# Banks for the first q and u, and the order of work at the change of row blocks, in a fused GELU feed-forward forward and backward kernel

## The chip, the cores and the metric

The kernel runs on one core of one Trainium2 chip, as a single launch. Its time is device microseconds (us) of that core; the number compared is the median of repeated runs. Beside the times there is one profiled execution, from which all durations of single instructions come.

## The reference

One feed-forward layer with an approximate (tanh) GELU, and its gradients, in bf16:

```python
h   = x @ w1 + b1            # x [2048, 448], w1 [448, 1792]
out = gelu(h) @ w2 + b2      # w2 [1792, 448]
# vjp with grad_out [2048, 448]:
gh  = (grad_out @ w2.T) * gelu'(h)
gx  = gh @ w1.T;  gw1 = x.T @ gh;  gb1 = sum(gh)
gw2 = gelu(h).T @ grad_out;        gb2 = sum(grad_out)
```

The outputs are out, gx, gw1, gb1, gw2 and gb2.

## The kernel before

The 2048 rows are four blocks of 512 (`NB`), the 1792 hidden columns seven pairs of 128-wide tiles (`NPAIR`). One **step** g is one pair of hidden tiles in one row block, so there are 28 steps and seven steps to a block; step 7 is the first of block 1. All is transposed: hidden columns lie on the partitions, rows along the free dimension. The order of instructions on each engine is the order in which the Python code issues them (a manual schedule); the engines meet only through semaphores, which the tile framework puts in where a tile is written after a read or read after a write.

In a step g the engines do this, by the names that the profile's lines use:

- TensorE makes `u` = w1.T x for step g+2 (`M1`, L239, six matmuls, and L249 in `rest`, one 64-row matmul for each half), `q` = w2 grad_out.T for step g (L252 in `rest`, then `M4`, L258, six matmuls), and between them **pieces** (L406): single matmuls of the out and gx products, each for one `Unit`, which is 128 rows of out ("o") or gx ("g") and accumulates over 14 pieces.
- ScalarE (`act_first`, `act_second`) copies u with its bias into `V` (L285, two instructions, which free u), squares it into `A` (L286), writes gelu into `hT` (L287), and takes tanh of `Bt` (L357). It also evicts some units (L420).
- VectorE (`dve_first`, `dve_second`, `dve_gate`) makes `Bt` from A and V (L354), p from A and hT (L361), adds constants to t and p (L362, L363), multiplies them (L364), and the **gate** multiplies by q into `ghT` (L375), which frees q. It also evicts the other units of out, adding b2 (L422).
- GpSimd issues the stores of finished units (L426) and of hT to a DRAM scratch (L379), and makes a few copies (L163). SyncE issues the loads and the transposes of ghT.

PSUM has eight banks of 128 x 512 float32: `psum_u` holds one tile `u` of two banks, `psum_g` one tile `q` of two banks, `psum_a` four tiles `acc` of one bank. The pools have one, one and four buffers, so that the next u waits until ScalarE has copied the last one, the next q until the gate has read the last one, and a new accumulator until one of four is evicted or read. V, A and Bt exist once. V may be written again when Bt has been made.

Step 0 is cut into two halves of 256 rows, so that it can begin when half of x has landed. `first_products` makes its u: the first half in two acc tiles, the second half in one q tile (`ub`, two banks). `first_chain` runs ScalarE (L311 copy, L316, L320, L323) and VectorE (L312 copy, L326, L330, L332, L335, L336) over the halves. Then TensorE issues M1 and rest of step 1, three matmuls that keep it busy (L279), and `first_q` (L271): one q tile whose two banks hold the two row halves, with one more such matmul between them. The gate of step 0 (L371) is two instructions, one for each half, on that one tile.

Block 0 has four out units under way (`grow[0]`), whose accumulators are finished at step 6, the last of block 0. Units 0 and 1 are evicted by ScalarE at step 6, after the pieces; units 2 and 3 by VectorE at step 7, ahead of the gate. At step 7 the kernel runs four pieces of two new out units (`grown`), then M1 of step 9, then eight pieces of gx (`own`):

```python
        flush(False); dve_gate(g); act_first(nxt); flush(True); dve_first(nxt)
        act_second(nxt); dve_second(nxt)
        if g == NPAIR:
            run_pieces(grown); M1(g + 2); run_pieces(own)
```

From step 6 on, each step ends with up to two stores of hT. After the 28 steps the last block's units are finished, and the weight gradients follow (L569, L577, L588), with the sums for gb1 and gb2 on VectorE and GpSimd.

Of the kernel before, what the change touches and what calls it, by code (L numbers as in the profile page):

```python
# [11 lines left out]
F32 = mybir.dt.float32  # L12
# [6 lines left out]
def kernel(  # L19
# [15 lines left out]
    nc = tc.nc  # L35
    P = 128
# [10 lines left out]
    SB = 512  # L47
    NB = S // SB
    SPB = SB // P
    NPAIR = NF // 2  # L50
    assert DL == 64 and F % 256 == 0 and S % SB == 0 and NPAIR == 7 and NB == 4
    NSTEP = NB * NPAIR
# [11 lines left out]
    psum_u = ctx.enter_context(tc.tile_pool(name="psum_u", bufs=1, space=bass.MemoryType.PSUM))  # L64
    psum_g = ctx.enter_context(tc.tile_pool(name="psum_g", bufs=1, space=bass.MemoryType.PSUM))
    psum_a = ctx.enter_context(tc.tile_pool(name="psum_a", bufs=4, space=bass.MemoryType.PSUM))
# [23 lines left out]
    w2T_sb = w2T_flat.rearrange("p (k f) -> p k f", k=KD)  # L90
# [12 lines left out]
    def gq(b):  # L103
        o = ((b % 2) * 2 + 1) * KD * SB
        return xg_flat[:, o:o + KD * SB].rearrange("p (k s) -> p k s", k=KD)
# [5 lines left out]
    def hT(g):  # L111
        return ring(hT_flat, HR, g)
# [4 lines left out]
    def V_of(g):  # L117
        return VA_flat[:, 0:2 * SB].rearrange("p (h s) -> p h s", h=2)

    def A_of(g):  # L120
        return VA_flat[:, 2 * SB:4 * SB].rearrange("p (h s) -> p h s", h=2)
# [4 lines left out]
    def t_of(g):  # L126
        return ring(T_flat, 4, 2 * (g % 2))

    def p_of(g):
        return ring(T_flat, 4, 2 * (g % 2) + 1)  # L130
# [8 lines left out]
    HB = SB // 2  # L139
# [84 lines left out]
    def cols(g, h):  # L224
        c = g % NPAIR
        return slice((2 * c + h) * P, (2 * c + h + 1) * P)

    u_of = {}
    g_of = {}

    def M1(g):
        if g == 0:
            u_of[g] = [psum_a.tile([P, SB], F32, name="acc")[:] for h in range(2)]
        else:
            u = psum_u.tile([P, 2, SB], F32, name="u")
            u_of[g] = [u[:, h, :] for h in range(2)]
        for h in range(2):
            for kt in range(KF):
                nc.tensor.matmul(u_of[g][h], lhsT=w1_sb[:, 1 + kt, cols(g, h)], rhs=xq(g // NPAIR)[:, 1 + kt, :],  # L239
                                 start=(kt == 0), stop=False, skip_group_check=True)  # L240
# [20 lines left out]
    def first_q():  # L261


        q = psum_g.tile([P, 2, SB], F32, name="q")
        g_of[0] = q
        for r in range(2):
            rs = slice(r * HB, (r + 1) * HB)
            for kt in (KF, *range(KF)):
                ps = slice(0, DL if kt == KF else P)
                for h in range(2):  # L270
                    nc.tensor.matmul(q[:, r, h * HB:(h + 1) * HB], lhsT=w2T_sb[ps, kt, cols(0, h)], rhs=gq(0)[ps, kt, rs],  # L271
                                     start=(kt == KF and h == 0), stop=(kt == KF - 1),
                                     tile_position=(0, 0) if kt == KF else None, skip_group_check=True)
            if r == 0:
                keep_warm(1, w1_sb[:, 1, 0:P], xq(0)[:, 1, :])
# [2 lines left out]
        for i in range(n):  # L278
            nc.tensor.matmul(pw[:], lhsT=weights, rhs=moving, start=True, stop=True)  # L279

    def act_first(g):
        u = u_of.pop(g)
        for h in range(2):
            ft = 2 * (g % NPAIR) + h
            nc.scalar.activation(out=V_of(g)[:, h, :], in_=u[h], func=ACT.Identity, bias=b1_col[:, ft:ft + 1])  # L285
        nc.scalar.activation(out=A_of(g), in_=V_of(g), func=ACT.Square, scale=math.sqrt(3.0 * GELU_C * GELU_A))  # L286
        nc.scalar.activation(out=hT(g), in_=V_of(g), func=ACT.Gelu_apprx_tanh)  # L287

    def first_products():

        ub = psum_g.tile([P, 2, SB], F32, name="q")
        u_of[0] = [[psum_a.tile([P, SB], F32, name="acc")[:, 0:HB] for h in range(2)], [ub[:, h, 0:HB] for h in range(2)]]
        for r in range(2):
            rs = slice(r * HB, (r + 1) * HB)
            for h in range(2):
                for kt in range(KF):
                    nc.tensor.matmul(u_of[0][r][h], lhsT=w1_sb[:, 1 + kt, cols(0, h)], rhs=xq(0)[:, 1 + kt, rs],
                                     start=(kt == 0), stop=False, skip_group_check=True)
            for h in range(2):
                nc.tensor.matmul(u_of[0][r][h], lhsT=w1_sb[DL:P, 0, cols(0, h)], rhs=xq(0)[DL:P, 0, rs],  # L300
                                 start=False, stop=True, tile_position=(DL, 0), skip_group_check=True)
            if r == 0:
                keep_warm(1, warm[:, 0:P], warm)
# [52 lines left out]
    def act_second(g):  # L356
        nc.scalar.activation(out=t_of(g), in_=B_of(g), func=ACT.Tanh, scale=-1.0 / 3.0)  # L357


    def dve_second(g):  # L360
        nc.vector.scalar_tensor_tensor(out=p_of(g), in0=A_of(g), scalar=GELU_C, in1=hT(g), op0=ALU.add, op1=ALU.mult)  # L361
        nc.vector.tensor_scalar(out=t_of(g), in0=t_of(g), scalar1=1.0, scalar2=None, op0=ALU.add)  # L362
        nc.vector.tensor_scalar(out=p_of(g), in0=p_of(g), scalar1=-0.5, scalar2=None, op0=ALU.add)  # L363
        nc.vector.tensor_tensor(out=t_of(g), in0=t_of(g), in1=p_of(g), op=ALU.mult)  # L364

    def dve_gate(g):
        q = g_of.pop(g)
        if g == 0:
            for r in range(2):
                rs = slice(r * HB, (r + 1) * HB)  # L370
                nc.vector.scalar_tensor_tensor(out=ghT(g)[:, :, rs], in0=t_of(g)[:, :, rs], scalar=1.0,  # L371
                                               in1=q[:, r, :].rearrange("p (h s) -> p h s", h=2),
                                               op0=ALU.add, op1=ALU.mult)
        else:
            nc.vector.scalar_tensor_tensor(out=ghT(g), in0=t_of(g), scalar=1.0, in1=q[:], op0=ALU.add, op1=ALU.mult)  # L375
# [38 lines left out]
    def evict(un):  # L414
        key = (un.kind, un.b, un.j // 2)
        if key not in stage:
            stage[key] = iop.tile([P, 2, D], BF16, name="io_" + un.kind)
        st = stage[key]
        if un.by_act:
            nc.scalar.copy(out=st[:, un.j % 2, :], in_=un.ps[:, 0:D])  # L420
        else:
            nc.vector.tensor_tensor(out=st[:, un.j % 2, :], in0=un.ps[:, 0:D], in1=b2_bc[:], op=ALU.add)  # L422
        dst = out2 if un.kind == "o" else gx2
        if un.j % 2:
            r0 = row0(un.b) + (un.j - 1) * P
            nc.gpsimd.dma_start(out=dst[r0:r0 + 2 * P, :].rearrange("(j p) d -> p j d", p=P), in_=st[:])  # L426

    full = []

    def run_pieces(units):  # L430
        for un in units:
            if un.piece():
                full.append(un)

    def flush(by_act=None):
        for un in [un for un in full if by_act in (None, un.by_act)]:
            full.remove(un)
            evict(un)


    U = {(k, b, j): Unit(k, b, j) for k in "og" for b in range(NB) for j in range(SPB)}
    seq = {
# [30 lines left out]
    for g in range(NSTEP):  # L473
        b, c = blk(g)
        pieces = [U[k] for k in seq[b] for _ in range(NF)]
        n = len(pieces)
        own = pieces[n * c // NPAIR:n * (c + 1) // NPAIR]
        grown = [U[k] for k in grow[b] for _ in range(2)]
        nxt = g + 1 if g + 1 < NSTEP else None
        if g > 0:  # L480
            rest(nxt, g)
            M4(g)
        flush(False)
        dve_gate(g)
        if nxt is not None:
            act_first(nxt)
        flush(True)
        if nxt is not None:
            dve_first(nxt)
        last = b == 0 and c == NPAIR - 1  # L490
        if last:
            run_pieces(grown + own)
            flush(True)
        if nxt is not None:
            act_second(nxt)
            dve_second(nxt)
        if g == NPAIR:
            run_pieces(grown)
            M1(g + 2)
            run_pieces(own)  # L500
        elif not last:
            run_pieces(grown + own)
        if g != NPAIR and g + 2 < NSTEP:
            M1(g + 2)
        for _ in range(2):
            if g >= NPAIR - 1 and stored < g:
                store_h(stored)
                stored += 1
        if c == 2 and 0 < b < NB - 1:
            load_x(b + 1)  # L510
            load_g(b + 1)
        for t in turns.get(g, []):
            turn_gh(*t)
# [8 lines left out]
    for k in "og":  # L522
        for j in range(SPB):
            un = U[k, NB - 1, j]
# [6 lines left out]
    for ft in range(NF):  # L531
        t = slots[ft].rearrange("p (s f) -> p s f", s=NS)
# [27 lines left out]
    for t0, t1 in ((0, 4), (4, HT)):  # L560
        n = (t1 - t0) * P
        for h in range(2):
            a0, a1 = t0 + h * HT, t1 + h * HT
            cs = slice(a0 * P, a1 * P)
            for kt in range(KF):
                ps = psum_a.tile([P, SB], F32, name="acc")
# [61 lines left out]
```

## Time and profile before

| what | us |
|---|---|
| median of three runs | 275.34 (275.0 to 275.69) |
| the profiled execution | 275.51 |
| its span, first to last instruction | 273.7 |
| TensorE matmuls busy | 267.9 (98%) |
| VectorE busy | 191.1 (70%) |
| ScalarE busy | 144.1 (53%) |
| GpSimd busy | 53.5 (20%) |

The profile gives for each instruction its start and duration from the beginning of the span, the engine (PE is TensorE, PEld its weight loads, DVE VectorE, ACT ScalarE, POOL GpSimd, SP SyncE; a q behind the name is the engine's sequencer), the source line, the operation, the tile written and the tiles read. In the list in order of time, neighbouring instructions of one kind are one row with a count; its duration is that of them all. A bracket at the end says how long the engine sat idle before the row, and what ended that. In the list of waits, a row has the waiting instruction, what it waited for, the microseconds in total, how often, and the longest. Matmuls overlap: a 512-column matmul has a bar of about 0.38 us, while the next one starts 0.216 us later.

### The profile page before, as it was taken

Reading aid. Unit: us, or ns where it says so; the run is one execution under the profiler, and the core shown is the slowest. Engines: PE = TensorE matmul, PEld = TensorE weight load, DVE = VectorE, ACT = ScalarE, POOL = GpSimd, SP = SyncE. Lnnn points to the kernel's source line nnn. Section 1 sums busy time; section 2 is a strip of 40 time slices with the busy share of each in tenths; the row PEclk is TensorE's granted clock in tenths of the full one; section 3 lists DMA queues with packets and bytes.
Section 4 is the critical chain, followed back from the end, with each engine's and each line's share of the span. In section 5 each row is a group of like instructions: output and inputs, shape, how many; then the busy total and the mean of one; then the engine's idle time right before and its main releaser. Section 6 shows DMA issues by size and latency. Waiting matters only on the chain.

```text
span 273.7 us, 3611 instructions
## 1 busy us (share of the span) xinstructions
PE 267.9 (98%) x1407; PEld 124.7 (46%) x1407; DVE 191.1 (70%) x229; ACT 144.1 (53%) x191; POOL 53.5 (20%) x59
## 2 busy tenths in 40 slices
PE   7999999999999999999999999999999999999995
PEld 3444434444444344444444445554445555555552
DVE  2799999999999999999888871149999970000000
ACT  3968879788988778887777740011111221112111
POOL 0000002830301503033031137111700029300000
PEclk9999999999999999999999999999999999999999
DMA  7999999999579927255534339999999931101111
GB/s 158 197 278 236 153 208 180 305 155 315 125 169 220 251 58 149 37 154 124 137 111 79 110 103 217 273 359 243 174 235 244 240 101 57 44 9 50 50 51 36
DMA packets 101533, 43.78 MB, mean 160 GB/s; under 512 B 90092, under 2 KB 98156, under 8 KB 101516
## 3 DMA queue, kind: packets, MB, share of 16 engines
q1 hardware_dynamic: 94432, 26.91, 52.8%
q0 software_dynamic: 4512, 14.69, 17.1%
q10 hardware_dynamic: 2572, 1.95, 2.3%
q8 instruction: 11, 0.18, 0.3%
q14 instruction: 6, 0.05, 0.1%
HBM read 7.00 MB, written 14.23 MB: 78 GB/s over the span
## 4 chain that ended last, share of the span: by engine, by line
PE 82%; DVE 12%; SPq 2%; DMA 2%; ACT 0%; issue 0%; DVEq 0%
PE acc L406 27%; PE acc L588 16%; PE acc L569 13%; PE q L258 10%; PE u L239 9%; PE u L249 4%; DVE T L361 3%; DVE Bt L354 3%; DVE ghT_h L375 3%; PE acc L577 2%; DMA w2T_g<-in_w_dram 2%; DVE T L364 2%; SPq L145 1%; DVE T L362 1%; PE q L271 1%; DVE T L363 1%
## 5 line engine op out<-in xcount | busy, mean ns | idle before, releaser
L406 PE MATMUL acc<-w_gw,hT_h 128*128 128x448 bf16 x224 | 46.3, 353 | 0.0
L406 PE MATMUL acc<-w1T_gw,ghT_h 128*128 128x448 bf16 x224 | 45.1, 353 | 0.0
L285 ACT ACTIVATE VA<-u,b_col 128x512 f32<-128x512 f32 x54 | 33.9, 679 | 13.3 <-PE u L249 13.3
L239 PE MATMUL u<-xg_h,w_x 128*128 128x512 bf16 x162 | 39.4, 379 | 0.7 <-ACT VA L285 0.6
L258 PE MATMUL q<-xg_h,w2T_g 128*128 128x512 bf16 x162 | 39.7, 381 | 0.0
L375 DVE SCALAR_TENSOR_TENSOR ghT_h<-T,q 128x1024 bf16<-128x1024 bf16 x27 | 33.0, 1220 | 7.9 <-PE q L258 6.6
L569 PE MATMUL acc<-gh_nat,w_x 128*128 128x512 bf16 (+1 forms) x192 | 36.7, 353 | 0.0
L357 ACT ACTIVATE T<-Bt 128x1024 bf16<-128x1024 f32 x27 | 28.5, 1057 | 14.6 <-DVE Bt L354 14.5
L361 DVE SCALAR_TENSOR_TENSOR T<-VA,hT_h 128x1024 bf16<-128x1024 f32 x27 | 33.1, 1227 | 0.0
L354 DVE SCALAR_TENSOR_TENSOR Bt<-VA 128x1024 f32<-128x1024 f32 x27 | 32.9, 1219 | 0.0
L406 PEld LDWEIGHTS <-hT_h 128*128 128x128 bf16 x224 | 21.9, 98 | 21.4
L406 PEld LDWEIGHTS <-ghT_h 128*128 128x128 bf16 x224 | 21.9, 98 | 20.9
L554 DVE TENSOR_TENSOR VA<-VA,gh_nat 128x1792 f32<-128x1792 f32 x14 | 30.0, 2142 | 0.5
L286 ACT ACTIVATE VA<-VA 128x1024 f32<-128x1024 f32 x27 | 28.5, 1057 | 0.9
L287 ACT ACTIVATE hT_h<-VA 128x1024 bf16<-128x1024 f32 x27 | 28.1, 1040 | 0.0
L569 PEld LDWEIGHTS <-w_x 128*128 128x128 bf16 x192 | 18.7, 98 | 17.8 <-issue 0.4
L258 PEld LDWEIGHTS <-w2T_g 128*128 128x128 bf16 x162 | 13.6, 97 | 24.2 <-issue 11.4
L239 PEld LDWEIGHTS <-w_x 128*128 128x128 bf16 x162 | 15.8, 98 | 18.7 <-issue 0.8
L590 ACT CAST w_gw<-acc 128x448 bf16<-128x448 f32 x13 | 6.9, 532 | 32.6 <-PE acc L588 32.6
L571 ACT CAST w1T_gw<-acc 128x512 bf16<-128x512 f32 (+1 forms) x12 | 6.3, 532 | 30.1 <-PE acc L569 27.4
L379 POOL DMA_DIRECT2D hT_dram<-hT_h x28 | 20.4, 729 | 0.1
L420 ACT CAST io_g<-acc 128x448 bf16<-128x448 f32 x16 | 8.3, 520 | 22.6 <-PE acc L406 22.6
(74 smaller groups left out, 241.0 us busy)
## 6 DMA issues: line engine op xcount, KB each, us to landing
hT_dram<-hT_h POOLq DMA_DIRECT2D x28, 256.0 KB, 4.2
out_dram<-io_o POOLq DMA_DIRECT2D x8, 224.0 KB, 4.3
out_dram<-io_g POOLq DMA_DIRECT2D x8, 224.0 KB, 3.4
w_x<-in_x_dram POOLq DMA_DIRECT2D x1, 1344.0 KB, 10.9
w2T_g<-in_grad_out_dram POOLq DMA_DIRECT2D x1, 1344.0 KB, 14.2
out_dram<-w_gw SPq DMA_DIRECT2D x4, 336.0 KB, 2.4
w_x<-in_w_dram SPq DMA_DIRECT2D x2, 384.0 KB, 4.5
out_dram<-w1T_gw ACTq DMA_DIRECT2D x2, 384.0 KB, 4.3
```

The source lines that it names most:

```text
L239: nc.tensor.matmul(u_of[g][h], lhsT=w1_sb[:, 1 + kt, cols(g, h)], rhs=xq(g // NPAIR)[:, 1 + kt, :], start=(kt == 0), stop=False, skip_grou ...
L258: nc.tensor.matmul(g_of[g][:, h, :], lhsT=w2T_sb[:, kt, cols(g, h)], rhs=gq(g // NPAIR)[:, kt, :], start=False, stop=(kt == KF - 1), skip_ ...
L285: nc.scalar.activation(out=V_of(g)[:, h, :], in_=u[h], func=ACT.Identity, bias=b1_col[:, ft:ft + 1])
L286: nc.scalar.activation(out=A_of(g), in_=V_of(g), func=ACT.Square, scale=math.sqrt(3.0 * GELU_C * GELU_A))
L354: nc.vector.scalar_tensor_tensor(out=B_of(g), in0=A_of(g), scalar=3.0 * GELU_C, in1=V_of(g), op0=ALU.add, op1=ALU.mult)
L357: nc.scalar.activation(out=t_of(g), in_=B_of(g), func=ACT.Tanh, scale=-1.0 / 3.0)
L361: nc.vector.scalar_tensor_tensor(out=p_of(g), in0=A_of(g), scalar=GELU_C, in1=hT(g), op0=ALU.add, op1=ALU.mult)
L375: nc.vector.scalar_tensor_tensor(out=ghT(g), in0=t_of(g), scalar=1.0, in1=q[:], op0=ALU.add, op1=ALU.mult)
L406: nc.tensor.matmul(self.ps[:, 0:D], lhsT=lhsT, rhs=rhs, start=(ft == 0), stop=(ft == NF - 1 and not bias))
L554: nc.vector.tensor_tensor(out=gsb_v, in0=gsb_v, in1=gh_rows(st, 0, NF), op=ALU.add)
L569: nc.tensor.matmul(psv, lhsT=x_all[:, st, kt * P:(kt + 1) * P], rhs=gh_rows(st, a0, a1), start=(st == 0), stop=(st == NS - 1))
L588: nc.tensor.matmul(ps[:, 0:D], lhsT=h_blk[ft][:, st, :], rhs=g_all[:, st, :], start=(st == 0), stop=(st == NS - 1))
```

## The change

Two places change.

At the start, the two row halves of the first q are two tiles of psum_a instead of one tile of psum_g, and the gate of step 0 reads them one by one. The second half of the first u lies in the first bank of a psum_u tile (which ScalarE copies) and the first bank of a psum_g tile (which VectorE copies), instead of both banks of one psum_g tile.

At the change of blocks, ScalarE's work on u is split into the copies (`act_copy`) and the rest (`act_rest`), VectorE's second part into p (`dve_p`) and the rest (`dve_rest`), and `take(j)` evicts one unit. Step 6 ends with the eviction of unit 0 alone; its tanh and what follows on VectorE move into step 7. There ScalarE does the copies of step 8, tanh of step 7, unit 1, then square and gelu of step 8. VectorE does p, unit 2, the constants and product, the gate, unit 3, then Bt of step 8. TensorE does three pieces of gx, M1 of step 9, the five other pieces of gx, and then the four pieces of out. The store of units 0 and 1 is issued in step 7, behind the first two stores of hT.

```diff
     def first_q():
-        q = psum_g.tile([P, 2, SB], F32, name="q")
-        g_of[0] = q
+        g_of[0] = []
         for r in range(2):
             rs = slice(r * HB, (r + 1) * HB)
+            q = psum_a.tile([P, SB], F32, name="acc")
+            g_of[0].append(q)
             for kt in (KF, *range(KF)):
                 ps = slice(0, DL if kt == KF else P)
                 for h in range(2):
-                    nc.tensor.matmul(q[:, r, h * HB:(h + 1) * HB], lhsT=w2T_sb[ps, kt, cols(0, h)], rhs=gq(0)[ps, kt, rs],
+                    nc.tensor.matmul(q[:, h * HB:(h + 1) * HB], lhsT=w2T_sb[ps, kt, cols(0, h)], rhs=gq(0)[ps, kt, rs],
...
-    def act_first(g):
+    def act_copy(g):
         u = u_of.pop(g)
         for h in range(2):
             ft = 2 * (g % NPAIR) + h
             nc.scalar.activation(out=V_of(g)[:, h, :], in_=u[h], func=ACT.Identity, bias=b1_col[:, ft:ft + 1])
+
+    def act_rest(g):
         nc.scalar.activation(out=A_of(g), in_=V_of(g), func=ACT.Square, scale=math.sqrt(3.0 * GELU_C * GELU_A))
         nc.scalar.activation(out=hT(g), in_=V_of(g), func=ACT.Gelu_apprx_tanh)
...
-        ub = psum_g.tile([P, 2, SB], F32, name="q")
-        u_of[0] = [[psum_a.tile([P, SB], F32, name="acc")[:, 0:HB] for h in range(2)], [ub[:, h, 0:HB] for h in range(2)]]
+        ub = [psum_u.tile([P, 2, SB], F32, name="u"), psum_g.tile([P, 2, SB], F32, name="q")]
+        u_of[0] = [[psum_a.tile([P, SB], F32, name="acc")[:, 0:HB] for h in range(2)], [t[:, 0, 0:HB] for t in ub]]
...
-    def dve_second(g):
+    def dve_p(g):
         nc.vector.scalar_tensor_tensor(out=p_of(g), in0=A_of(g), scalar=GELU_C, in1=hT(g), op0=ALU.add, op1=ALU.mult)
+
+    def dve_rest(g):
         nc.vector.tensor_scalar(out=t_of(g), in0=t_of(g), scalar1=1.0, scalar2=None, op0=ALU.add)
...
-                                               in1=q[:, r, :].rearrange("p (h s) -> p h s", h=2),
+                                               in1=q[r].rearrange("p (h s) -> p h s", h=2),
...
+    def take(j):
+        un = full[[u.j for u in full].index(j)]
+        full.remove(un)
+        evict(un)
...
-        flush(False)
-        dve_gate(g)
-        if nxt is not None:
-            act_first(nxt)
-        flush(True)
+        last = b == 0 and c == NPAIR - 1
+        if g == NPAIR:
+
+            act_copy(nxt)
+            act_second(g)
+            dve_p(g)
+            take(2)
+            dve_rest(g)
+            dve_gate(g)
+            take(1)
+            take(3)
+            act_rest(nxt)
+        else:
+            flush(False)
+            dve_gate(g)
+            if nxt is not None:
+                act_copy(nxt)
+                act_rest(nxt)
+            flush(True)
         if nxt is not None:
             dve_first(nxt)
-        last = b == 0 and c == NPAIR - 1
         if last:
             run_pieces(grown + own)
-            flush(True)
-        if nxt is not None:
+            take(0)
+        elif nxt is not None:
             act_second(nxt)
-            dve_second(nxt)
+            dve_p(nxt)
+            dve_rest(nxt)
         if g == NPAIR:
-            run_pieces(grown)
+            run_pieces(own[:3])
             M1(g + 2)
-            run_pieces(own)
-        elif not last:
-            run_pieces(grown + own)
-        if g != NPAIR and g + 2 < NSTEP:
-            M1(g + 2)
+            run_pieces(own[3:] + grown)
+        else:
+            if not last:
+                run_pieces(grown + own)
+            if g + 2 < NSTEP:
+                M1(g + 2)
```

## The prediction

> **What bounds the kernel now.** I read the page first, then the waits of TensorE, then the order of time in two places: the first 20 us, and the change from row block 0 to row block 1 near 45 us.
>
> ```profile
> span 273.7 us, 3611 instructions
> ...
> PE 267.9 (98%) x1407; PEld 124.7 (46%) x1407; DVE 191.1 (70%) x229; ACT 144.1 (53%) x191; POOL 53.5 (20%) x59
> ```
>
> TensorE is busy for 98% of the span, so only what shortens TensorE's idle time, or lengthens it, moves the end. The waits of TensorE, complete:
>
> ```profile
> PE acc L279 <- DVE T L185: 1.2, 1, 1.2
> PE u L239 <- ACT VA L285: 0.6, 1, 0.6
> PE q L271 <- DMA w2T_g<-in_w_dram: 0.5, 1, 0.5
> PE acc L297 <- DMA xg_h<-in_x_dram: 0.2, 1, 0.2
> ```
>
> Only the second and third belong to code that the change touches. The start, in order of time (start, duration, engine, line):
>
> ```profile
> 7.37 1.47 PE L239 MATMUL u<-xg_h,w_x 128*128 128x512 bf16 x6
> ...
> 7.62 0.45 ACT L311 ACTIVATE VA<-q,b_col 128x256 f32<-128x256 f32 x1
> 8.11 0.48 DVE L312 TENSOR_SCALAR VA<-q,b_col 128x256 f32<-128x256 f32 x1 [0.19 <-ACT VA L311]
> ...
> 10.65 1.15 PE L271 MATMUL q<-xg_h,w2T_g 64*128 64x256 bf16 x8 [0.53 <-DMA w2T_g<-in_w_dram]
> ...
> 13.14 1.28 DVE L371 SCALAR_TENSOR_TENSOR ghT_h<-T,q 128x512 bf16<-128x512 bf16 x2 [0.77 <-PE q L271]
> ...
> 16.41 1.47 PE L258 MATMUL q<-xg_h,w2T_g 128*128 128x512 bf16 x6
> ...
> 17.48 0.69 DVE L364 TENSOR_TENSOR T<-T 128x1024 bf16<-128x1024 bf16 x1
> ...
> 18.28 1.22 DVE L375 SCALAR_TENSOR_TENSOR ghT_h<-T,q 128x1024 bf16<-128x1024 bf16 x1
> ```
>
> In block 0 VectorE is the slow engine: its gates (L375) come every 5.07 us (18.28, 23.35), while TensorE's step takes 4.75 us (L258 at 16.41, then 21.16). VectorE therefore falls 0.3 us a step behind, and TensorE pays at the end of the block:
>
> ```profile
> 39.66 0.39 PE L249 MATMUL u<-xg_h,w_x 64*128 64x512 bf16 x1
> ...
> 39.96 0.37 PE L252 MATMUL q<-xg_h,w2T_g 64*128 64x512 bf16 x1
> ...
> 44.90 1.22 DVE L354 SCALAR_TENSOR_TENSOR Bt<-VA 128x1024 f32<-128x1024 f32 x1
> ...
> 46.15 1.06 ACT L357 ACTIVATE T<-Bt 128x1024 bf16<-128x1024 f32 x1
> ...
> 47.12 1.25 ACT L285 ACTIVATE VA<-u,b_col 128x512 f32<-128x512 f32 x2
> ...
> 48.41 1.46 PE L239 MATMUL u<-xg_h,w_x 128*128 128x512 bf16 x6 [0.58 <-ACT VA L285]
> ...
> 49.71 1.21 DVE L375 SCALAR_TENSOR_TENSOR ghT_h<-T,q 128x1024 bf16<-128x1024 bf16 x1
> ...
> 50.82 4.41 POOL L379 DMA_DIRECT2D hT_dram<-hT_h  x6
> ...
> 53.52 0.83 DVE L363 TENSOR_SCALAR T<-T 128x1024 bf16<-128x1024 bf16 x1
> ```
>
> L249 and L252 start together in other steps; at 39.66 L252 comes 0.30 late, for the gate that ends at 38.69 + 1.22 = 39.91 still holds q. No wait list shows this 0.30. So 0.30 + 0.58 = 0.88 us of TensorE time lies at the end of block 0.
>
> **The start, step by step.** (1) The second half of u now has one tile in psum_u, which the next u needs. L239 of step 1 must wait until ScalarE has copied it: 7.62 + 0.45 = 8.07, plus 0.04 as at 48.37 to 48.41, so 8.11 instead of 7.37, 0.74 late. Behind it stand L249, three warming matmuls and the first q. That q stands 0.53 (by bars) behind its neighbour, or 0.61 by issue (three matmuls of 0.216 from 9.31, and 0.08). TensorE is late by 0.13 to 0.21; I take 0.13, as issue, not bars, sets the pace in all later steps.
>
> (2) VectorE's copy no longer waits for ScalarE's. The operation before it ends at 7.91, neighbours overlap by 0.08: it starts at 7.83, 0.28 earlier, and the whole chain to t*p ends at 12.08 instead of 12.36.
>
> (3) The gate of step 0 comes in halves. The second half still needs the last q matmul, 13.10 + 0.13 = 13.23, so it ends near 13.95 instead of 14.42: VectorE is 0.47 ahead.
>
> (4) But the gate of step 1 needs M4, which ends at 16.41 + 1.47 + 0.13 = 18.01. It starts at 18.05 instead of 18.28, and VectorE's lead is cut to 0.23. ScalarE doesn't cut it further: its copy of step 2 becomes 0.06 later at most, and A is ready before Bt asks for it.
>
> (5) Added waits: the third and fourth accumulators of step 0 now take the banks of the two q halves. TensorE reaches them at about 13.86 and 14.24; the half gates end at 12.8 and 13.95. They cost nothing while that cover of 0.25 us lasts, and as much as it is overrun.
>
> At step 6 TensorE then arrives at 39.66 + 0.13 = 39.79, after the gate has freed q (39.91 - 0.23 + 0.04 = 39.72). The 0.30 is gone, the 0.13 stays: TensorE is **0.17 ahead**.
>
> **The change of blocks.** (6) The copies of u go ahead of tanh, behind Bt of step 7, which ends at 46.12 - 0.23 = 45.89. They run from 45.92 to 47.17. TensorE does three pieces first, 46.74 to 47.31, and finds u free: the 0.58 is gone. Were that all, it would reach q of step 8 0.75 early, at 51.32 - 0.75 = 50.57.
>
> (7) tanh is what pays: queued behind the copies it runs 47.09 to 48.15, 0.94 late. Behind it VectorE's two T operations (0.34 apart), t*p at 48.98 to 49.67, and after the usual 0.11 the gate, 49.78 to 50.99. Leaving one eviction (0.58) for after the gate doesn't make it up: the gate ends 0.07 later than before. q of step 8 (L252) waits for it until 51.03. The lead shrinks to 51.32 - 51.03 = **0.29**.
>
> (8) The eviction moved behind the gate (0.53 net) and Bt of step 8 follow: Bt starts near 51.44 instead of 50.84, 0.60 late. The gate of step 8 ended at 56.41, of which 0.41 was one long L363 (0.83 against a median of 0.42). It now ends at 56.60, and q of step 9 starts at 56.64, while TensorE arrives at 51.03 + 5.50 = 56.53. Before it was 56.82. The lead is **0.18**. From here VectorE's 5.07 against TensorE's 5.50 opens 0.4 us a step, and nothing further waits; TensorE has no later wait to fill, so 0.18 reaches the end.
>
> (9) GpSimd's queue: the first io_o store now stands behind the first two hT stores, which before waited for it until 47.39. They follow the copy of w2T_g and run near 31.0 to 32.5. Their 512 KB meet loads whose users come much later (g of block 1, issued from 31.69, is read at 45.07): no cost. But L362 and L363 of step 4 lie beside them, and those of step 8 beside the other six.
>
> What such a meeting costs, the rows bound: 0.41 once (53.52), 0 at 47.58. The copy at 30.48 may also stop lengthening L361 (1.42 against 1.23), a gain of 0.2. In (8) there is no slack left, so every such delay moves the end. Bounds of the sum: -0.18 - 0.20 = -0.38 and -0.18 + 2 x 0.41 = +0.64. I take -0.15, near the undelayed rows, since most L363 keep the median.
>
> [...]
>
> **Sum.** The profiled execution took 275.51 us, 273.7 of it span and 1.8 around it; the change makes 275.36 of it. That execution stands 0.17 above the median 275.34, so I forecast a median of 275.2. About 0.3% (0.83 us) is what a measurement of this kernel can tell from no change.
>
> **The rivals.** *The whole gain reaches the end* (0.14): VectorE keeps the full 0.47 and the start costs TensorE nothing, so 0.30 + 0.58 arrives: 275.34 - 0.88 = 274.46. For it: both waits really go. Against it: (4) and (7), in which another engine ends last by 0.3 to 0.5 us.
>
> *VectorE meets GpSimd's stores more than once* (0.25): at step 4 and step 8, +0.64, 275.98; a third meeting, or one of 0.73, passes 276.17. It decides as soon as the delays together exceed 0.18 + 0.83 = 1.0 us. I give 0.14 of the 0.25 to that.
>
> *TensorE slows after its new gap at the start* (0.06), slower: the first eight matmuls take 0.43 each (1.18 to 4.61), later ones 0.216. The gap in (1) is 0.87 us, from 7.24. If matmuls fell back to the slow rate for as long as that first stretch, 3.4 us, half of it, 1.7, is lost: 275.2 + 1.7 = 276.9. Against it: the gap of 0.53 at 10.12 left the pace unchanged. [...]
>
> **Numbers.** My forecast as worked out has 0.55, within 0.3%. Same: 0.55 + 0.11 = 0.66; faster 0.14; slower 0.14 + 0.06 = 0.20. The range runs from the whole gain, 274.4, to just past the double meeting, 276.2; beyond lie the slowed clock and the heavier meetings.
>
> **What would show it.** Right: L239 of step 1 at 8.1; gate halves ending near 12.8 and 13.95; gate of step 1 near 18.05; L249 and L252 together at step 6; no wait at L239 near 47.3; instead q of step 8 waiting some 0.4 us for the gate near 51.0, and Bt of step 8 near 51.4. Wrong: q of step 8 starting near 50.6, a gate of step 8 ending past 57.1, or matmuls at 0.43 after 8 us.

## The result, and the profile after

| | median us | lowest to highest | runs |
|---|---|---|---|
| before | 275.36 | 274.87 to 275.73 | 22 |
| after | 275.92 | 275.45 to 276.65 | 22 |

The ratio after to before is 1.0022, 95% interval [1.0015, 1.0029]: the change costs about 0.6 us. The profiled execution of the changed kernel took 276.14 us, 0.22 above its median. Its page begins:

```profile
span 274.4 us, 3612 instructions
...
PE 268.5 (98%) x1407; PEld 125.1 (46%) x1407; DVE 191.5 (70%) x229; ACT 143.8 (52%) x191; POOL 55.1 (20%) x59
```

TensorE is again busy for 98%, and the span grew by 0.7. The waits of TensorE, without the one at the very start that both kernels have:

```profile
PE u L239 <- ACT VA L314: 0.9, 1, 0.9
PE acc L300 <- DMA xg_h<-in_x_dram: 0.3, 1, 0.3
PE q L252 <- DVE ghT_h L380: 0.3, 1, 0.3
```

The wait of the first q for w2T and the wait of L239 at the change of blocks are gone, as foreseen. In their place stand the wait of L239 of step 1 for ScalarE's copy, now 0.9 long, and one of q for the gate. The start in order of time (L314 is ScalarE's copy, L272 the first q, L376 the gate of step 0, L380 the gate of later steps):

```profile
6.40 0.47 ACT L314 ACTIVATE VA<-acc,b_col 128x256 f32<-128x256 f32 x1 [2.39 <-PE acc L303]
...
8.15 0.45 ACT L314 ACTIVATE VA<-u,b_col 128x256 f32<-128x256 f32 x1
...
8.65 1.46 PE L239 MATMUL u<-xg_h,w_x 128*128 128x512 bf16 x6 [0.88 <-ACT VA L314]
...
11.33 1.15 PE L272 MATMUL acc<-xg_h,w2T_g 64*128 64x256 bf16 x8
...
13.81 0.69 DVE L376 SCALAR_TENSOR_TENSOR ghT_h<-T,acc 128x512 bf16<-128x512 bf16 x1 [0.59 <-PE acc L272]
...
17.05 1.47 PE L258 MATMUL q<-xg_h,w2T_g 128*128 128x512 bf16 x6
...
18.56 1.22 DVE L380 SCALAR_TENSOR_TENSOR ghT_h<-T,q 128x1024 bf16<-128x1024 bf16 x1 [0.31 <-PE q L258]
```

The first q starts at 11.33, 0.68 later than the 10.65 of before, and waits for no load. The second gate half follows the last q matmul, and the gate of step 1 follows M4, so VectorE's pace too now hangs on the first q: its gate of step 1 starts 0.28 later than before (18.56 against 18.28). The change of blocks (L360 is tanh, L367 and L368 VectorE's constants, L357 Bt, L364 p, L384 the stores of hT, L163 GpSimd's copy for row block 2):

```profile
47.76 1.06 ACT L360 ACTIVATE T<-Bt 128x1024 bf16<-128x1024 f32 x1
...
48.85 0.43 DVE L367 TENSOR_SCALAR T<-T 128x1024 bf16<-128x1024 bf16 x1 [0.69 <-ACT T L360]
...
50.44 1.22 DVE L380 SCALAR_TENSOR_TENSOR ghT_h<-T,q 128x1024 bf16<-128x1024 bf16 x1
...
51.02 0.39 PE L249 MATMUL u<-xg_h,w_x 64*128 64x512 bf16 x1
51.72 0.37 PE L252 MATMUL q<-xg_h,w2T_g 64*128 64x512 bf16 x1 [0.31 <-DVE ghT_h L380]
...
53.22 4.33 POOL L384 DMA_DIRECT2D hT_dram<-hT_h  x6
...
57.20 0.39 PE L249 MATMUL u<-xg_h,w_x 64*128 64x512 bf16 x1
57.35 0.37 PE L252 MATMUL q<-xg_h,w2T_g 64*128 64x512 bf16 x1
...
57.55 1.34 POOL L163 COPY xg_h<-xg_h 64x512 bf16<-64x512 bf16 x1
58.35 1.63 DVE L364 SCALAR_TENSOR_TENSOR T<-VA,hT_h 128x1024 bf16<-128x1024 f32 x1
...
59.90 0.64 DVE L367 TENSOR_SCALAR T<-T 128x1024 bf16<-128x1024 bf16 x1
...
62.84 0.39 PE L249 MATMUL u<-xg_h,w_x 64*128 64x512 bf16 x1
62.98 0.37 PE L252 MATMUL q<-xg_h,w2T_g 64*128 64x512 bf16 x1
```

Read L249 and L252 as a pair: where L252 starts later than L249, TensorE stood waiting for the gate. It stands 0.70 at step 8, 0.15 at step 9 and 0.14 at step 10. Before, the three pairs were together (51.31 and 51.32, 56.82 twice, 62.32 twice) and the 0.58 at L239 took the place of the 0.70. Some rows of the kernel before for comparison (L311 is ScalarE's copy there, L361 p):

```profile
5.87 0.47 ACT L311 ACTIVATE VA<-acc,b_col 128x256 f32<-128x256 f32 x1 [1.82 <-PE acc L300]
...
51.31 0.39 PE L249 MATMUL u<-xg_h,w_x 64*128 64x512 bf16 x1
51.32 0.39 PE L252 MATMUL q<-xg_h,w2T_g 64*128 64x512 bf16 x1
...
55.23 0.62 POOL L163 COPY xg_h<-xg_h 64x512 bf16<-64x512 bf16 x1
...
57.46 1.22 DVE L361 SCALAR_TENSOR_TENSOR T<-VA,hT_h 128x1024 bf16<-128x1024 f32 x1
```

From step 11 on the changed kernel is a steady 0.64 late (68.47 against 67.83).

### The profile page after: what moved, and what is told of

It is laid out like the page before. It is cut to its first block, busy times and chain, and to the rows that moved or that the text cites. A ratio compares the mean times of both kernels' runs of the same rounds, so it can differ in the third digit from the quotient of the medians.

```text
span 274.4 us, 3612 instructions
## 1 busy us (share of the span) xinstructions
PE 268.5 (98%) x1407; PEld 125.1 (46%) x1407; DVE 191.5 (70%) x229; ACT 143.8 (52%) x191; POOL 55.1 (20%) x59
## 4 chain that ended last, share of the span: by engine, by line
PE 84%; DVE 11%; DMA 2%; ACT 2%; issue 0%; DVEq 0%; ACTq 0%
PE acc L411 27%; PE acc L613 15%; PE acc L594 13%; PE q L258 11%; PE u L239 9%; PE u L249 4%; DVE ghT_h L380 3%; DVE Bt L357 2%; PE acc L602 2%; DVE T L364 2%; DMA xg_h<-in_x_dram 2%; DVE T L369 2%; DVE T L367 1%; DVE T L368 1%; PE acc L272 1%; PE q L252 1%
## 5 line engine op out<-in xcount | busy, mean ns | idle before, releaser
L239 PE MATMUL u<-xg_h,w_x 128*128 128x512 bf16 x162 | 39.4, 379 | 0.9 <-ACT VA L314 0.9
L380 DVE SCALAR_TENSOR_TENSOR ghT_h<-T,q 128x1024 bf16<-128x1024 bf16 x27 | 32.9, 1220 | 7.2 <-PE q L258 5.7
L360 ACT ACTIVATE T<-Bt 128x1024 bf16<-128x1024 f32 x27 | 28.5, 1057 | 17.7 <-DVE Bt L357 17.5
L364 DVE SCALAR_TENSOR_TENSOR T<-VA,hT_h 128x1024 bf16<-128x1024 f32 x27 | 33.5, 1241 | 0.0
L357 DVE SCALAR_TENSOR_TENSOR Bt<-VA 128x1024 f32<-128x1024 f32 x27 | 32.9, 1219 | 0.1
L239 PEld LDWEIGHTS <-w_x 128*128 128x128 bf16 x162 | 15.8, 98 | 18.6 <-issue 1.0
L384 POOL DMA_DIRECT2D hT_dram<-hT_h x28 | 20.5, 733 | 0.0
```

The costliest lines, as they stand in the source:

```text
L357: nc.vector.scalar_tensor_tensor(out=B_of(g), in0=A_of(g), scalar=3.0 * GELU_C, in1=V_of(g), op0=ALU.add, op1=ALU.mult)
```

## The experiments

"Start" is the part in `first_q` and `first_products`, "blocks" the part at the change of row blocks. All times are medians; the differences in the last column are (ratio - 1) x 275.4.

| kernel | us | runs | ratio to before | difference |
|---|---|---|---|---|
| start alone | 275.63 | 12 | 1.0008 [0.9998, 1.0017] | +0.2 |
| blocks alone | 275.74 | 11 | 1.0011 [1.0002, 1.0019] | +0.3 |
| q halves alone | 275.00 | 11 | 0.9986 [0.9977, 0.9994] | -0.4 |
| gx pieces first alone | 275.02 | 11 | 0.9985 [0.9976, 0.9993] | -0.4 |
| q halves and gx first | 274.74 | 8 | 0.9977 [0.9967, 0.9987] | -0.6 |
| changed, u's second half as before | 275.49 | 11 | 1.0002 [0.9993, 1.0011] | +0.1 |
| changed, hT stores later | 276.21 | 11 | 1.0023 [1.0014, 1.0032] | +0.6 |
| blocks alone, tanh first | 275.84 | 11 | 1.0013 [1.0004, 1.0022] | +0.4 |
| q halves, tanh first, gx first | 274.55 | 5 | 0.9968 [0.9956, 0.9980] | -0.9 |
| blocks alone, unit 3 by ScalarE | 275.50 | 11 | 1.0002 [0.9994, 1.0011] | +0.1 |
| blocks alone, load of block 2 earlier | 275.74 | 12 | 1.0016 [1.0001, 1.0030] | +0.4 |
| start alone, copy ahead of gelu | 275.44 | 11 | 0.9997 [0.9988, 1.0005] | -0.1 |

### The two parts alone

Start alone takes the edits in `first_q` and `first_products` (and the gate's `q[r]`), with everything else as before; blocks alone is the rest of the diff.

> Only the start of the change: q halves and u's second half in tiles of their own; the change of blocks is as before. Theory A (the wait for w2T at the first q, 0.53 us, was the cover for a late start, and the new wait of L239 for ScalarE's copy uses it up, so that late starts now reach the end): slower than before by 0.2 to 0.5 us, TensorE reaching the first q at 10.8 or later and the times more spread. Theory B (the start is worth what the prediction's sum says, and the loss lies at the change of blocks): faster than before by about 0.2 us.

> Only the change of blocks; the start is as before. Theory A: within 0.2 us of before, since the wait of 0.58 at L239 is exchanged for a wait of about 0.5 at q of step 8 and some 0.1 at step 9. Theory B: slower than before by 0.4 to 0.7 us, with waits of TensorE for the gate at steps 8, 9 and 10.

Measured: +0.2 and +0.3. Together they make 0.5, within the noise the 0.6 of the whole, so the loss is divided, and neither theory had all of it. The interval of the start alone runs from no change to +0.5: the gain of 0.2 that theory B gave it is out, the loss of theory A is not yet shown by this run alone. The interval of the change of blocks, from 0.05 to 0.5, reaches both theories.

The traces show the price of the change of blocks more sharply, because the stretch from q of step 7 to q of step 10 leaves the start out. It takes 17.24 us before (45.08 to 62.32) and with the start alone (44.78 to 62.02), but 17.53 with the blocks alone (45.00 to 62.53) and in the changed kernel (45.45 to 62.98): 0.29 for the change of blocks. In the changed kernel q of step 7 comes 0.37 later than before; that much of its 0.64 was there already.

### Half of the start: the q halves, and the u tiles

```diff
-        q = psum_g.tile([P, 2, SB], F32, name="q")
+        q = psum_a.tile([P, SB], F32, name="acc")     # one for each half
...
         ub = psum_g.tile([P, 2, SB], F32, name="q")   # u's second half: as before
```

> Only the q halves in tiles of their own; u's second half stays in one q tile, so that L239 of step 1 waits for no copy; the change of blocks is as before. Theory A: TensorE starts the first q at the landing of w2T as before, VectorE leads by 0.36 us (gate of step 1 at 17.9), the 0.30 at step 6 goes and the wait at L239 shrinks: 0.3 to 0.4 us faster than before, and 0.5 us or more faster than with u's tiles split. Theory B: as the start alone, about 0.2 us faster; no difference of more than 0.2 between this and the start alone.

Measured: 275.00, so the q halves gain 0.4. Between this kernel and the start alone lies only the second half of u in tiles of its own: 1.0008 - 0.9986 = 0.0022, or 0.6 us, and the two intervals do not overlap. The reverse test takes the whole change and undoes just those tiles:

```diff
-        ub = [psum_u.tile([P, 2, SB], F32, name="u"), psum_g.tile([P, 2, SB], F32, name="q")]
+        ub = psum_g.tile([P, 2, SB], F32, name="q")
```

> The changed kernel with one edit undone: the second half of the first u lies in the two banks of one psum_g tile, as before, so that L239 of step 1 has no copy of ScalarE to wait for. Theory A (the wait of L239 is what the start costs, about 0.6 us, and it goes through to the end): about 275.3 us, equal to the kernel before; the idle time of 0.88 ahead of L239 is gone, first q near 10.5, and all later q 0.6 earlier than in the changed kernel. Rival (the gate of step 7 sets the time, whatever TensorE does before): TensorE comes 0.6 earlier and waits 0.6 longer at L252 of step 8 (51.27 with the change of blocks alone), and the time stays at 275.7 or above.

Measured: 275.49, 0.0020 x 275.4 = 0.55 us less than the changed kernel, again with intervals apart. Theory A holds: the gap ahead of L239 is gone in its trace, and the gain goes through to the end.

The profile of the start alone looks harmless, with its first q at 10.73 against 10.53 with the q halves alone. Its profiled execution took 275.19, though, 0.44 under that kernel's median. Set side by side, the starts of all fourteen profiled executions show why (start times in us; "first copy" is ScalarE's copy of u's first half):

| u's second half | kernel | first copy | L239 of step 1 | first q | q after copy | q of step 7 after copy |
|---|---|---|---|---|---|---|
| one tile | blocks alone | 5.81 | 7.11 | 10.49 | 4.68 | 39.19 |
| | before | 5.87 | 7.37 | 10.65 | 4.78 | 39.21 |
| | q halves alone | 5.89 | 7.62 | 10.53 | 4.64 | 38.69 |
| | blocks, tanh first | 6.00 | 7.57 | 10.51 | 4.51 | 38.92 |
| | blocks, load earlier | 6.09 | 7.43 | 10.12 | 4.03 | 38.45 |
| | q halves, tanh and gx first | 6.12 | 7.51 | 10.35 | 4.23 | 38.42 |
| | gx first alone | 6.16 | 7.46 | 10.24 | 4.08 | 38.50 |
| | q halves and gx first | 6.30 | 7.60 | 10.38 | 4.08 | 38.38 |
| | blocks, unit 3 by ScalarE | 6.34 | 7.64 | 10.33 | 3.99 | 38.41 |
| | changed, u as before | 6.59 | 7.89 | 10.58 | 3.99 | 38.38 |
| own tiles | start alone | 5.81 | 8.06 | 10.73 | 4.92 | 38.97 |
| | changed | 6.40 | 8.65 | 11.33 | 4.93 | 39.05 |
| | changed, stores later | 6.60 | 8.85 | 11.52 | 4.92 | 38.97 |
| own tiles, copy ahead of gelu | start alone | 6.72 | 8.64 | 11.32 | 4.60 | 38.65 |

The start varies from one execution to the next: the first copy comes anywhere between 5.81 and 6.72. With u's second half in one tile, a late start is swallowed: q comes between 10.12 and 10.65 whatever the copy does. After the four earliest copies, up to 6.00, q waits for the load of w2 (0.62, 0.53, 0.15 and 0.17) and starts at 10.49 to 10.65; after the six later ones, from 6.09 on, it waits for no load and starts as early as 10.12, so there the load had even landed sooner. With tiles of its own, L239 needs ScalarE's second copy, and q is tied to the first copy at a fixed distance of 4.92. The mean of the fourteen copies is 6.19; 6.19 + 4.92 = 11.11, against a mean of 10.42 for the ten with one tile: 0.69 at the first q by the traces, 0.55 and 0.6 by the times.

Two pairs of traces with like starts need no mean. The first rows are of the changed kernel with u's second half as before, the second of the changed kernel with the stores later (ScalarE's first copy, then q of step 7; the first q of each is in the table):

```profile
6.59 0.47 ACT L314 ACTIVATE VA<-acc,b_col 128x256 f32<-128x256 f32 x1 [2.54 <-PE acc L303]
...
44.97 0.39 PE L252 MATMUL q<-xg_h,w2T_g 64*128 64x512 bf16 x1
```

```profile
6.60 0.47 ACT L314 ACTIVATE VA<-acc,b_col 128x256 f32<-128x256 f32 x1 [2.58 <-PE acc L303]
...
45.57 0.39 PE L252 MATMUL q<-xg_h,w2T_g 64*128 64x512 bf16 x1
```

After a late copy, then, tiles of its own put the first q 0.94 later, and 0.60 of it is left at q of step 7. After an early copy (start alone at 5.81, q halves alone at 5.89) they put the first q 0.20 later (10.73 against 10.53), and q of step 7 as well (44.78 against 44.58).

The gain of the q halves hangs on the start too, which the last column of the table shows for the ten kernels with one tile. After an early copy q of step 7 comes 38.92 to 39.21 after it without the q halves, and 38.69 with them; after a late one 38.41 to 38.50 without, and 38.38 to 38.42 with them.

### The distance itself changed

```diff
         copy(0); square(0)
-        gelu(0)
         cubic(0); copy(1)
+        gelu(0)
```

> The kernel with the start alone, with ScalarE's copy of u's second half ahead of its gelu of the first half (0.45 long). Theory A (with u in tiles of its own, the first q comes a fixed 4.92 after ScalarE's first copy, because L239 waits for the second copy, and that costs 0.6 on average): the second copy comes 0.4 earlier, q 4.5 after the first copy, and 0.3 to 0.4 of the 0.6 returns: about 275.3 instead of 275.63. Rival (the loss has nothing to do with that wait): q follows the load of w2 as before, and the time stays at 275.6; or, if gelu's delay holds up VectorE's chain, gate of step 0 is late and it grows.

The start of this kernel in order of time (L312 is ScalarE's copy):

```profile
8.12 0.47 ACT L312 ACTIVATE VA<-u,b_col 128x256 f32<-128x256 f32 x1
...
8.64 1.46 PE L239 MATMUL u<-xg_h,w_x 128*128 128x512 bf16 x6 [0.45 <-ACT VA L312]
```

The gap ahead of L239 is halved, from 0.88 to 0.45, q comes 4.60 after the first copy instead of 4.92, and q of step 7 38.65 after it instead of 38.97: the 0.32 goes through. By the ratios 0.0011 x 275.4 = 0.3 us of the 0.6 returns, the low end of what was expected. In the trace, moving the cause moves the effect, and as far; the times go the same way, but their intervals overlap and would not show it alone.

### GpSimd's first stores

```diff
-            if g >= NPAIR - 1 and stored < g:
+            if g >= NPAIR and stored < g:
```

> The changed kernel with the first two hT stores issued behind the store of units 0 and 1 again, as in the kernel before, so that GpSimd runs nothing beside VectorE's constants of step 4 near 31 us. If the meeting with these stores is what delays VectorE (theory B2), the gate of step 7 comes some 0.3 earlier than at 50.44 and the time falls by 0.2 to 0.4, to about 275.6. If the order of tanh and copies is what delays it (theory B1) or the wait at the start is all (theory A), nothing changes: 275.9, within 0.1 of the changed kernel, with the gate of step 7 at 50.3 to 50.5.

Measured: 1.0023 against the changed kernel's 1.0022, gate of step 7 at 50.55. It follows a first q 0.19 later than in the changed kernel, so relative to q it moved by 0.08. Theory B2, as far as the stores at step 4 go, falls.

### tanh and the copies

```diff
+            act_second(g)
             act_copy(nxt)
-            act_second(g)
```

> The kernel with the change of blocks alone, with one edit: tanh of step 7 again ahead of ScalarE's two copies of u, units still taken out one at a time. If tanh's place behind the copies is what cost the 0.3 us of that kernel (theory B1), the gate of step 7 returns to about 49.7 and the loss goes: 275.4 or below, though L239 may show a wait of 0.3 to 0.6 for the copies again. If the copies' early place is worth more than it costs (the sum of the prediction), the kernel becomes slower than the 275.74 of the change of blocks alone: about 276.0, with the wait at L239 back and no wait at L252 of step 8.

Measured: no better than blocks alone, 1.0013 against 1.0011. One of its eleven executions took 400.63 us, far from the other ten (275.54 to 276.16); what happened there is not known, and the median does not feel it. In its trace the gate of step 7 is early (49.14) and all pairs of L249 and L252 are together, so VectorE is out of the way; instead L239 of step 9 waits 0.77 for the copies. Before, it waited 0.58 with one more piece ahead of it, 0.19. Wait and piece make the same sum, and with one piece fewer hidden in the wait, one more follows it: the step from the pair of step 7 to that of step 8 takes 6.44 (44.92 to 51.36) instead of 6.24. Theory B1 had the gate right and the time wrong: whichever of ScalarE's jobs goes first, the other's user waits, VectorE 0.69 for tanh, or TensorE 0.77 for the copies. From q of step 7 to q of step 10 this kernel takes 17.44, between the 17.53 of blocks alone and the 17.24 of before.

### More work for TensorE ahead of M1

This is the kernel before with one edit, `own` being the eight gx pieces.

```diff
         if g == NPAIR:
-            run_pieces(grown)
-            M1(g + 2)
             run_pieces(own)
+            M1(g + 2)
+            run_pieces(grown)
```

> Another cure for the wait of 0.58 at L239: the kernel before, with one edit at step 7, the eight gx pieces ahead of M1 of step 9 and the four out pieces behind it; tanh, copies and evictions stay as before. Both theories that blame tanh's place or GpSimd's stores expect the wait at L239 to go, q of step 8 to wait for the gate until 50.96 instead of starting at 51.32, and VectorE's later gates to stay where they are: 0.36 us faster than before. If it is not faster, something else than tanh's place sets the start of step 8.

> The kernel before with two edits that each gained about 0.4 alone: the halves of the first q in tiles of their own (u's second half left in one tile), and at step 7 the eight gx pieces ahead of M1 of step 9. If they remove separate losses (0.42 at the start, 0.40 at the change of blocks), the sum arrives: ratio 0.997, about 274.6 us, q of step 9 near 55.8. Rival: both shift the same meeting, the gate of step 7 against TensorE; then TensorE comes early at step 7, waits there for the gate, and the two together bring no more than one alone: about 275.0. In that case L252 of step 8 shows a stall of 0.3 or more, and q of step 9 starts near 56.05 or later.

Measured: -0.4 and -0.6. Eight pieces cover the 0.58 for the copies without touching ScalarE's order; from q of step 7 to q of step 10 the gx pieces first alone take 16.89 instead of 17.24. With the q halves added, the interval of the times, 0.4 to 0.9, holds both the sum of 0.8 and the gain of one edit alone, so it decides nothing. The trace has what the rival asked for: L249 of step 8 starts at 50.18 and L252 at 50.57, a stall of 0.39 for the gate, and q of step 9 starts at 56.06. But the gx pieces first alone show the same (50.16 and 50.56, then 56.05), so this is no sign that the two edits meet there: the stretch takes 16.88 with both. Where the q halves gain little in this trace is ahead of step 7. Its start is late (first copy at 6.30), and there the halves bring about 0.1: 38.38 from first copy to q of step 7, against 38.50.

### VectorE behind the gate

Unit 3 is evicted by ScalarE behind gelu, a probe that leaves out b2 for that unit; in the other kernel the loads of row block 2, with GpSimd's copy for them, are issued ahead of the two stores of step 9.

```diff
             take(1)
-            take(3)
             act_rest(nxt)
+            take(3, True)              # by ScalarE
```

> The kernel with the change of blocks alone, unit 3 evicted by ScalarE behind its gelu instead of by VectorE behind the gate (b2 is left out of that unit). Theory (VectorE sets the time from step 7 to step 9: its eviction of 0.53 behind the gate makes the step from gate 7 to gate 8 5.63 long, and moves GpSimd's stores and its copy late): gate of step 8 near 55.1 instead of 55.63, the stalls of q at step 9 (0.14) and step 10 (0.14) gone, time about 275.45. Rival (the 0.3 of the change of blocks is no matter of VectorE's work behind the gate, but lies ahead of it, in the idle 0.69 for tanh): the stall ahead of q of step 8 stays, those behind it too, time 275.7.

```diff
+        if c == 2 and 0 < b < NB - 1:
+            load_x(b + 1); load_g(b + 1)
         for _ in range(2):
             ...                          # store_h
-        if c == 2 and 0 < b < NB - 1:
-            load_x(b + 1); load_g(b + 1)
```

> The kernel with the change of blocks alone, with the loads of the third row block, and so GpSimd's copy for it, issued ahead of the two hT stores of step 9 instead of behind them. Theory (the copy, pushed to 57.12 by the stores that wait for the late eviction, is what lengthens VectorE's L363 from 1.22 to 1.63 and L366 from 0.43 to 0.64 at step 9): the copy now comes near 55.7, beside the gate or Bt; L363 and L366 of step 9 return to 1.22 and 0.43, gate of step 9 near 60.7 instead of 61.25, the stall of 0.14 ahead of q of step 10 goes, time about 275.6. Rival (it is the stores, not the copy, or the copy lengthens whatever VectorE does beside it): another VectorE instruction grows by as much, the stall of step 10 stays, 275.75.

With unit 3 on ScalarE the gate of step 8 starts at 55.27 (the product ahead of it took 1.15 instead of 0.69, else it would be the 55.1 expected or earlier), the stalls behind step 8 shrink from 0.14 and 0.14 to 0.04 and 0.01, and the stretch from q of step 7 to q of step 10 takes 17.29, so 0.24 of the 0.29 are gone. The time falls by 0.0009 x 275.4 = 0.25 to that of before, though the two intervals overlap; the 0.70 ahead of q of step 8 stays, since it only replaces the old wait at L239. So in the traces VectorE's eviction behind the gate, with what it drags along in GpSimd's queue, is the price of the change of blocks.

The second kernel shows the share of what stands in GpSimd's queue, in order of time:

```profile
55.17 1.22 DVE L379 SCALAR_TENSOR_TENSOR ghT_h<-T,q 128x1024 bf16<-128x1024 bf16 x1
55.22 0.62 POOL L163 COPY xg_h<-xg_h 64x512 bf16<-64x512 bf16 x1
```

Beside the gate neither the copy (0.62) nor the gate (1.22) grows, the p of step 9 is back at 1.22, the gate of step 9 starts at 60.25, and the stall at step 10 is gone (61.93 and 61.94). The stretch takes 17.40, 0.13 less than with the blocks alone. That is the theory's trace. The times do not confirm it: with a range of 275.12 to 277.87 they can't tell 0.14 from nothing, and the ratio of 1.0016 leans on that one longest execution (by medians it is 275.74 against 275.46 of the kernel before beside it).

### A version that beats both

From the changed kernel: u's second half in one tile, tanh ahead of the copies, `run_pieces(own)` ahead of M1 and `grown` behind it.

> The changed kernel with three edits: u's second half in one psum_g tile as before; tanh of step 7 ahead of the two copies of u; all eight gx pieces ahead of M1 of step 9. Theory: at the change of blocks either VectorE stands idle for tanh (copies first) or TensorE waits for the copies (tanh first), unless TensorE has other work ahead of M1; with eight pieces there, both waits go. Expected: gate of step 7 near 48.8, wait at L239 of step 9 under 0.2, q of step 8 near 50.2 instead of 50.57 with the gx pieces ahead alone, time about 274.4, ratio 0.996. Rival: the eviction behind the gate (VectorE's 5.6 a step at steps 8 and 9) eats it again: q of step 9 waits for its gate, and the time is 274.7 or above, no better than the gx pieces ahead with the q halves.

```profile
46.38 1.68 PE L411 MATMUL acc<-w1T_gw,ghT_h 128*128 128x448 bf16 x8
...
47.89 1.46 PE L239 MATMUL u<-xg_h,w_x 128*128 128x512 bf16 x6
...
50.04 0.39 PE L249 MATMUL u<-xg_h,w_x 64*128 64x512 bf16 x1
50.04 0.39 PE L252 MATMUL q<-xg_h,w2T_g 64*128 64x512 bf16 x1
```

Eight pieces, then L239 without a wait, then L249 and L252 together: nothing is left of the waits at the change of blocks. At steps 9 and 10 the pairs are 0.11 and 0.14 apart, so the rival takes back part of it. From q of step 7 to q of step 10 it takes 16.73, 0.51 less than before. The time is 274.55, 0.9 us under before, the best of all that ran, by five runs; against the q halves with the gx pieces alone (0.9977) the intervals overlap.

## Why the prediction was wrong

The forecast was 275.2, a small gain; measured were 275.92 and a loss. The measured time lies inside the stated range, but on the other side of before.

**Step (1) failed by its size, and it is most of the error.** The mechanism is right: L239 waits for ScalarE's copy, which ends at 8.60, and starts at 8.65, 0.05 behind it. The 0.13 came from one execution, whose first copy was among the earliest (5.87) and whose load of w2 landed late; for such a start it is about right, as the start alone shows (first copy at 5.81, first q at 10.73, where the sum had 10.78). The cover of 0.53 was taken as a property of the kernel. But of the ten executions with one tile only the four with the earliest copies waited for that load at all; in the others nothing covers the new wait. By the times it costs 0.55 to 0.6, 0.4 to 0.5 more than the sum had, by traces with like starts 0.20 after an early copy and 0.60 after a late one.

**Steps (2), (3) and (5) hold.** VectorE's second copy follows ScalarE's first by 1.96 (6.40 to 8.36) instead of 2.24 (5.87 to 8.11), the 0.28 of step (2), the gate comes in halves, and no accumulator waits for them. Step 6's stall of 0.30 shrinks to 0.09 in the profiled execution and is zero in the start alone. That is the gain of the q halves, which the u tiles eat: 0.4 alone against a cost of 0.55 to 0.6. Step (4) holds as a mechanism, the gate of step 1 waits 0.31 for M4. But the cut was worked out from a q at 10.78; with q at 11.33 VectorE isn't 0.23 ahead but 0.28 behind (18.56 against 18.28).

**Steps (6) and (7) hold.** L239 at 47.92 has no wait. From first q to gate of step 7 the prediction had 49.78 - 10.78 = 39.00; measured were 50.44 - 11.33 = 39.11. Step (8) holds to 0.04: the stall at step 9 was to be 0.11 and is 0.15. In the sum, though, the lead from the start was to pay for it.

**Step (9) priced the wrong instruction.** It looked at the stores. Moving the first two cost or gained nothing that the times show, and beside the six VectorE's constants of step 8 took 0.46 and 0.41, against 0.43 and 0.42. The gain of 0.2 that it thought possible at p of step 4 did not come: p takes 1.42 there as before. Unnamed was GpSimd's copy for row block 2 (L163), which stands behind the six stores. The eviction behind the gate starts the stores at 53.22 instead of 50.82, and the copy moves from beside the gate (55.23, 0.62 long) to beside Bt and p. There p takes 1.63 instead of 1.22, and behind it L367, beside the next store, 0.64 instead of 0.43. So "nothing further waits" fails at step 9, whose gate comes 5.63 after the last one instead of 5.07, and q of step 10 waits another 0.14. Forecast -0.15, plus 0.45 for the start and 0.14 for the wait at step 10, makes 0.44 of the 0.6; the 0.11 by which the gate of step 7 came later than the sum had it is most of the rest, and too small for the times to tell.

**The rivals.** The whole gain did not arrive. The rival of several meetings gave 275.98, near what was measured, but that is luck: neither the stores nor a delay above 1.0 us on VectorE made it. A meeting that costs 0.73, the length of one store's issue, is shown by no run: the longest delay of VectorE seen beside a store is 0.46 (the product of 1.15 instead of 0.69, unit 3 by ScalarE). The slowed clock is out: after the gap of 0.88 the six matmuls of L239 take 1.46, against 1.47 before, and the mean clock granted in that execution is 1.000.

## What to carry to other kernels

A gap that waits for a load at the start may stand only in some executions, here in four of the ten with one tile: before spending it on a new wait, look at the start in several executions, since one trace shows one draw. When an eviction is moved behind a gate, follow its store into the issuing engine's queue and on to whatever compute stands behind it there. And when two consumers wait for one engine's order, reordering that engine only chooses who waits, here VectorE 0.69 or TensorE 0.77; giving the consumer other work ahead of the wait, here eight pieces, removes it.

## What the runs showed of the hardware that was not expected

The same loads at the start let ScalarE's first copy begin between 5.81 and 6.72 in fourteen executions, a spread of 0.9 us, as large as the largest effect studied here. What sets it was not tried.

Where a GpSimd copy of 64 x 512 ran beside VectorE's Bt or p, the one that started later took longer in the traces below. Beside the gate, which reads q from PSUM and T from SBUF, the copy takes 0.62 and the gate its usual 1.22 (before, at 55.23 and 55.19). In the changed kernel it starts during Bt, which reads two tiles from SBUF: Bt keeps its 1.22, the copy takes 1.34, and p, which also reads two and starts while the copy still runs, takes 1.63 instead of 1.22. Where the copy starts first, it keeps its time: 0.60 just ahead of a p of 1.66 (q halves and gx first, at 56.66 and 56.68), 0.62 just ahead of a Bt of 1.61 (unit 3 by ScalarE, at 56.31 and 56.41). That the two inputs from SBUF decide it fits these rows; no run tried it alone.

Beside GpSimd's issues of stores VectorE's instructions took longer only now and then. Beside six in a row, 0.72 each, the two constants took 0.46 and 0.41 in the changed kernel; in other executions a constant beside them took 0.83 instead of 0.42 (before, at 53.52) and a product 1.15 instead of 0.69 (unit 3 by ScalarE, at 54.02). What decides it is open.
